# Gateloop attention with a multiplicative FFN: score and state products as 32-column blocks, a second copy of v, and a new place for the weight looks

## The chip, the cores and the metric

The kernel runs on one core of one Trainium2 chip. The metric is the device time in microseconds of one launch, as the median of several runs. Three runs of the kernel before gave 569.23, 569.44 and 571.16 us, so its time is 569.44 us.

## What is computed

The input is q, k, v and a complex gate a = (a_re, a_im), each 4 x 8 x 768 x 48 (batch, heads, sequence, head size) in fp32, and four weight matrices in fp64. For each batch and head a 48 x 48 complex state is multiplied, row by row, by the gate of the step and gets k v^T added; the output is q times the real part of the state. The outputs of all heads, as rows of 384, then go through an FFN that multiplies two projections with each other:

```python
mag = sqrt(a_re * a_re + a_im * a_im)
a_re, a_im = (x * min(mag, 0.999) / (mag + 1e-6) for x in (a_re, a_im))
for t in range(S):
    new_re = ar * S_re - ai * S_im
    new_im = ar * S_im + ai * S_re
    S_re, S_im = new_re + outer(k[t], v[t]), new_im
    y[t] = q[t] @ S_re
x = y.transpose(0, 2, 1, 3).reshape(B * S, H * D)      # 3072 x 384
out = ((x @ w1) * (x @ w2)) @ w3 @ w_out               # 384 -> 1024 -> 1024 -> 384
```

## The kernel before, in words

The sequence of a batch is cut into two halves of 384 steps. A half is a unit; there are NU = 8 units, each with UC = 3 chunks of C = 128 steps, for all 8 heads. The cumulative product of the gates turns the recurrence into products of matrices: with the gates' running product folded into q and k, the output of a chunk is a causal score product times v plus q times the state at the chunk's start.

**Start.** w3 and w_out are turned from fp64 to fp32 on VectorE and ScalarE and multiplied with each other into w3o (`row_work`, `fuse`, L973), so that the FFN needs one matrix less; w1 and w2 follow (`w12_work`, `load_weight`, L873 to L887). The gates of unit 0 and the first products of unit 0 are worked in between. `load_v` is called when row `VLOAD` (3) of w3 is reached.

**A unit** (`unit`, `pieces`) works on these things:

- `gates(u + 1)` (L541): the gates of the next unit, a chain of steps that goes back and forth between ScalarE (L554: Ln, Exp, Arctan, Sin) and VectorE (L566 to L638: products and scans over time). It ends with `gR` (L634), k (L635), gA and q (L637, L638), and with DMAs that move these into head order as KL and QL (L648). `turn` needs gR and k; `scores` needs KL and QL. Near its end it calls `spread_v` (L520), two copies on ScalarE that bring v from the loaded tile `vr` into `V`, with 64 columns a head where 48 are data and 16 stay zero.
- `turn` (L664): the transposes `tp` (L671) of three 128 x 128 blocks and a copy on ScalarE into KT (L673).
- `state` (L714): for each of 8 heads a product kv (L721) with a stationary operand of 96 columns (real and imaginary parts of k) and 64 moving columns (v), then an addition on VectorE into T (L728), at the end of a unit also a multiplication by the decay (L734). The second unit of a batch needs only two of them.
- `scores` (L676): for 4 heads a product sc (L683) with 96 rows, 128 stationary columns (k) and 128 moving ones (q), into one PSUM bank; then VectorE copies the causal part into A with a mask (L685). Two such calls make a chunk. Two banks take turns.
- `outputs` (L691): y (L710), all in the narrow form of TensorE: the stationary operand has 32 columns, and four such blocks, with outputs on PSUM partitions 0, 32, 64 and 96, are issued one after another (`lanes`). ScalarE copies the result into xT (L712).
- the FFN of the unit before, in between as filling: `ffn_ab` (L737) with 96 instructions m (L744) and a multiplication on VectorE (L750); `ffn_out` (o, L831); and `out_pair` (p, L795), seven half-size products that replace eight for two blocks of rows.
- `look` (`check_weights`, L899): 42 steps that test whether the inputs are in the range for which the fast way is sound: 6 of the gates, 36 of the fp64 weights. A step is a DMA, then two or three passes on ScalarE (L918 to L921, or L527). `judge` (L979) adds up all tests and the end of the kernel reads the verdict; a general way (`general`) stands behind it and isn't taken here.

**Order.** PE's order is written out by hand (`manual_schedule`): it is the order of the calls in `unit` and in the main part. The other engines' order is set by a scheduler from the order of calls and from priorities. Each engine then works strictly in its order. All DMAs are issued by SP, one after another, also in the scheduler's order; one that must wait for its buffer holds up those behind it. In `unit` each call of a piece is followed by a step of `gates`, and each piece by a step of `look`:

```python
for i in range(n):
    for f in rest[first[i]:first[i + 1]] + p[i]:
        f()
        next(steps, None)
    next(look, None)
```

## Time and profile before

| what | value |
|---|---|
| median of 3 runs | 569.44 us |
| span of the profiled execution, first to last instruction | 566.8 us |
| its own time over the span | not recorded apart; the median lies 2.6 us above the span |
| mean granted TensorE clock | 0.995 |
| PE busy | 541.8 us, 3682 matmul instructions |
| VectorE / ScalarE / GpSimd busy | 335.8 / 345.9 / 3.5 us |
| m (L744) | 768 instructions, 135.0 + 134.3 us |
| sc (L683) | 384 instructions, 47.2 us |
| kv (L721) | 320 instructions, 30.0 us |
| y (L710) | 1408 instructions, 39.2 + 34.4 us, interleaved |
| V copies (L524) | 16, 10.5 us |
| DMA queue | 46720 packets, 84.06 MB |

The page of the profile is of one execution. Busy time of an engine is the union of its instructions' times; for PE the ends of matmuls are modelled, and matmuls overlap, so the start-to-start distances in the chain and the timeline say more than the busy times. In lines of the groups, "x384 | 45.7, 192 | 1.3" reads: 384 instructions, 45.7 us busy in all, 192 ns each on average, 1.3 us of idle time of the engine just before them, followed by what ended it. In the chain, each line is its start in us, its length in us, and what was running.

### The profile page before, as it was taken

What the parts mean: (1) busy time and instruction counts of PE and PEld (TensorE: products, weight loads), DVE (VectorE), ACT (ScalarE), POOL (GpSimd) and SP (SyncE); (2) the same over time, 40 slices, a digit from 0 to 9 for tenths busy, and PEclk for the clock granted to TensorE, in tenths of its full rate; (3) what the DMA queues carried; (4) which work ended last, traced back from release to release, by engine and by line L of the source; (5) the groups of instructions that cost most, each with busy time, mean ns of one, the idle gap of its engine ahead of it and who ended that gap; (6) DMA issues with size and microseconds to landing.
All of it is one profiled execution on the core that took longest, in us unless ns stands there. A gap on an engine that the chain in (4) does not pass through costs nothing.

```text
span 566.8 us, 9285 instructions
## 1 busy us (share of the span) xinstructions
PE 541.8 (96%) x3682; PEld 386.1 (68%) x3682; DVE 335.8 (59%) x511; ACT 345.9 (61%) x569; POOL 3.5 (1%) x9
## 2 busy tenths in 40 slices
PE   4697899999999999999999999999999999999995
PEld 2354775577566975688567966697568965796564
DVE  6998599927752677356742796255743696332121
ACT  6979856655662798458963899289965645101100
POOL 2000000000000000000000000000000000000000
PEclk9999999999999999999999999999999999999999
DMA  8996985780382447935593427754393104200001
GB/s 285 374 364 190 322 268 169 204 214 16 98 189 53 122 141 221 247 109 183 184 206 111 144 81 218 209 157 148 125 207 101 30 28 115 67 2 30 0 1 47
DMA packets 46772, 84.74 MB, mean 150 GB/s; under 512 B 4736, under 2 KB 36480, under 8 KB 45952
## 3 DMA queue, kind: packets, MB, share of 16 engines
q1 hardware_dynamic: 46720, 84.06, 50.6%
q8 instruction: 31, 0.51, 0.4%
q14 instruction: 21, 0.17, 0.1%
HBM read 60.42 MB, written 4.72 MB: 115 GB/s over the span
## 4 chain that ended last, share of the span: by engine, by line
PE 77%; ACT 9%; DVE 7%; DMA 3%; issue 2%; SPq 1%; DVEq 0%; ACTq 0%
PE m L744 40%; PE o L831 9%; PE p L795 9%; PE y L710 5%; PE sc L683 5%; PE kv L721 5%; PE tp L671 2%; ACT gZ L554 1%; DMA look<-in_w_dram 1%; ACT look L918 1%; ACT look L919 1%; PE f L973 1%; DMA im<-in_a_im_dram 1%; ACT gR L554 1%; ACT gA L554 1%
## 5 line engine op out<-in xcount | busy, mean ns | idle before, releaser
L744 PE MATMUL m<-xT,w1s 128*128 128x384 f32 x384 | 135.0, 488 | 0.1
L744 PE MATMUL m<-xT,w2s 128*128 128x384 f32 x384 | 134.3, 486 | 0.0
L744 PEld LDWEIGHTS m<-xT,w2s 128*128 128x128 f32 x384 | 73.0, 190 | 50.9
L744 PEld LDWEIGHTS m<-xT,w1s 128*128 128x128 f32 x384 | 71.2, 190 | 45.3 <-ACT xT L712 1.0
L750 DVE TENSOR_TENSOR ab<-m,a 128x384 f32<-128x384 f32 x64 | 35.2, 553 | 84.7 <-PE m L744 77.4
L749 ACT COPY a<-m 128x384 f32<-128x384 f32 x64 | 30.1, 474 | 53.5 <-PE m L744 52.3
L973 PE MATMUL f<-wo_s,w3s 128*128 128x384 f32 x128 | 47.7, 528 | 15.5 <-DVE wo_s L887 15.5
L831 PE MATMUL o<-w3o,ab 128*128 128x384 f32 x160 | 54.0, 487 | 0.0
L673 ACT COPY KT<-tp 128x384 f32<-128x384 f32 x40 | 33.6, 851 | 32.2 <-PE tp L671 32.1
L973 PEld LDWEIGHTS f<-wo_s,w3s 128*128 128x128 f32 x128 | 25.5, 206 | 35.2 <-DVE wo_s L887 18.6
L683 PE MATMUL sc<-QL,KL 96*128 96x128 f32 x384 | 47.2, 276 | 0.3 <-DVE A L685 0.3
L683 PEld LDWEIGHTS sc<-QL,KL 96*128 96x128 f32 x384 | 45.7, 192 | 1.3 <-DVE A L685 0.6
L685 DVE COPY_PREDICATED A<-causal,sc 128x512 f32<-128x512 int32 x48 | 34.6, 741 | 14.0 <-PE sc L683 13.6
L831 PEld LDWEIGHTS o<-w3o,ab 128*128 128x128 f32 x160 | 29.6, 190 | 18.7 <-issue 0.4
L728 DVE TENSOR_TENSOR T<-kv,T 96x512 f32<-96x512 f32 x16 | 11.0, 686 | 51.4 <-PE kv L721 51.4
L710 PE MATMUL y<-A,V 128*32 128x128 f32 x768 | 39.2, 275 | 0.0
L710 PEld LDWEIGHTS y<-A,V 128*32 128x32 f32 x768 | 32.9, 109 | 3.3 <-issue 1.4
L710 PE MATMUL y<-QL,T 96*32 96x128 f32 x640 | 34.4, 272 | 0.0
L877 ACT ACTIVATE low<-raw 128x384 uint16<-128x384 uint32 (+4 forms) x28 | 25.1, 902 | 11.1 <-DVE low L873 5.1
L721 PEld LDWEIGHTS kv<-V,KT 128*96 128x96 f32 x320 | 29.6, 165 | 3.1 <-issue 1.4
L795 PE MATMUL p<-To,So 128*128 128x192 f32 x168 | 31.6, 335 | 0.0
L721 PE MATMUL kv<-V,KT 128*96 128x64 f32 x320 | 30.0, 247 | 1.5 <-ACT KT L673 1.5
(114 smaller groups left out, 748.7 us busy)
## 6 DMA issues: line engine op xcount, KB each, us to landing
look<-in_w_dram SPq DMA_DIRECT2D x28, 512.0 KB, 3.9
raw<-in_w_dram SPq DMA_DIRECT2D x6, 1024.0 KB, 10.2
raw<-in_w_dram SPq DMA_DIRECT2D x8, 768.0 KB, 6.7
KL<-gR SPq DMA_DIRECT2D x24, 192.5 KB, 3.3
KL<-k SPq DMA_DIRECT2D x24, 192.5 KB, 3.8
re<-in_a_re_dram SPq DMA_DIRECT2D x24, 192.0 KB, 5.2
im<-in_a_im_dram SPq DMA_DIRECT2D x24, 192.0 KB, 3.2
k<-in_k_dram SPq DMA_DIRECT2D x24, 192.0 KB, 3.3
```

Source lines behind the costliest of these rows:

```text
L673: nc.scalar.copy(out=KT_t[u, c][:, :, :, x].rearrange("p h d f -> p f d h"), in_=tp.rearrange("p f (d h) -> p f d h", h=H))
L683: nc.tensor.matmul(out=sc[:, j], lhsT=KL[:, x * n + j, w], rhs=QL[:, x * n + j, w], start=True, stop=True)
L685: masked[:] = [nc.vector.copy_predicated(out=A[:, x * n:(x + 1) * n], data=sc, mask=causal.rearrange("p (h t) -> p h t", h=1).to_broadcast ...
L710: nc.tensor.matmul(out=o, lhsT=a, rhs=b, start=s0, stop=s1)
L721: nc.tensor.matmul(out=kv[:, hd], lhsT=KT[:, hd].rearrange("p d x f -> p (d x f)"), rhs=V[:, hd], start=True, stop=True)
L744: nc.tensor.matmul(out=m, lhsT=w[:, j * P // WB, f, j * P % WB:j * P % WB + P], rhs=xT_t[u][:, f], start=(f == 0), stop=(f == KD - 1))
L749: copied[:] = [nc.scalar.copy(out=a, in_=got[0])]
L750: nc.vector.tensor_tensor(out=ab_t[u][:, j], in0=got[1], in1=a, op=OP.mult)
L795: nc.tensor.matmul(out=m[p], lhsT=a[:, f], rhs=b[:, f], start=(f == 0), stop=(f == KH - 1))
L831: nc.tensor.matmul(out=m, lhsT=ab_t[u][:, f, t * P:(t + 1) * P], rhs=w3o[:, f], start=(f == 0), stop=(f == KF - 1))
L877: nc.scalar.activation(out=ends.bitcast(U16)[:, 0::2].rearrange("p (r m) -> p r m", r=r), in_=lo.bitcast(U32), func=AF.Copy, scale=2.0 ** -29)
L973: nc.tensor.matmul(out=sums[j], lhsT=w3_t[f][:, j * P:(j + 1) * P], rhs=w3_t["wo"][:, f], start=(f == 0), stop=(f == KF - 1))
```

## The change

It has four parts.

1. **Scores in blocks.** Each 128 x 128 score product is cut into four with 32 stationary columns each. Block s0 needs the query steps from s0 on alone, so the moving columns are 128, 96, 64 and 32. Each block's output goes to one of the four groups of 32 PSUM partitions, chosen so that the four heads of a call stand in four different groups. The rows of a head's scores so are rotated by 32 times its number modulo 4; the mask is laid out to match (now 8 bits, made once for four heads), the two score banks are fixed tiles that are zeroed at the start, and the rows of v in `V` are rotated in the same way.
2. **States in blocks.** Each 96-column state product is cut into three with 32 columns, in three groups. v comes unrotated from `vr`, with 48 moving columns where there were 64. T has three fixed tiles, zeroed once, and 48 columns of each head are written.
3. **v twice.** `vr` is loaded as before, but a unit's load is now called after the last state of the unit before. `turn_v` loads v a second time from memory, straight into `V`, rotated, head by head: 14 DMAs a unit with runs of 192 bytes. `spread_v` is gone.
4. **Looks.** A unit takes a look after each of its first four pieces alone (the last unit after every piece); the remaining ones are taken in the last FFN, and `judge` comes four calls before its end.

The diff, with the plain renamings left out:

```diff
@@ -427,8 +428,10 @@
     TT = S // 2
     UC = TT // C
     NU = 2 * B
+    LOOKS = 4
     AHEAD = [0, 0] + [4] * (NU - 2)
     LO, HI = 32, D - 32
+    SB, LANES = 32, C // 32
     LN_EPS = math.log(1e-6)
     PI = math.pi
     MIN_SQ, MAX_SQ = 1.126 ** 2, 2.0 ** 32 - 512
@@ -446,8 +449,7 @@
     singles = fast.enter_context(tc.tile_pool(name="singles", bufs=1))
     one = fast.enter_context(tc.tile_pool(name="one", bufs=1))
     two = fast.enter_context(tc.tile_pool(name="two", bufs=2))
-    three = fast.enter_context(tc.tile_pool(name="three", bufs=3))
-    ps_s = fast.enter_context(tc.tile_pool(name="ps_s", bufs=2, space=PSUM))
+    ps_s = fast.enter_context(tc.tile_pool(name="ps_s", bufs=1, space=PSUM))
     ps_v = fast.enter_context(tc.tile_pool(name="ps_v", bufs=2, space=PSUM))
     ps_m = fast.enter_context(tc.tile_pool(name="ps_m", bufs=4, space=PSUM))
@@ -455,13 +457,19 @@
     gate_pool = [one, None]
+    Sc = [ps_s.tile([P, LANES, C], FP, name=f"sc{i}") for i in range(2)]
+    for sc in Sc:
+        nc.vector.memset(sc, 0.0)
     Ab = [singles.tile([P, H, C], FP, name=f"A{i}") for i in range(2)]
     Vb = [singles.tile([P, UC, H, 64], FP, name=f"V{i}") for i in range(2)]
-    causal = singles.tile([P, C], I32, name="causal")
-    nc.gpsimd.iota(causal, pattern=[[1, C]], base=0, channel_multiplier=-1)
-    nc.vector.tensor_scalar(out=causal, in0=causal, scalar1=0, scalar2=None, op0=OP.is_ge)
+    causal = one.tile([P, LANES, C], I32, tag="q", name="causal")
+    nc.gpsimd.iota(causal, pattern=[[SB, LANES], [1, C]], base=0, channel_multiplier=-1)
+    for j in range(1, LANES):
+        nc.vector.tensor_scalar(out=causal[0:SB * j, j], in0=causal[0:SB * j, j], scalar1=-C, scalar2=None, op0=OP.add)
+    mask = singles.tile([P, LANES, C], U8, name="mask")
+    nc.vector.tensor_scalar(out=mask, in0=causal, scalar1=0, scalar2=None, op0=OP.is_ge)
     consts = singles.tile([P, 7], FP, name="consts")
     for i, x in enumerate((1.0, LN_EPS, PI / 2, SMALL, -LARGE, MIN_SQ, -MAX_SQ)):
         nc.vector.memset(consts[:, i:i + 1], x)
@@ -506,8 +514,6 @@
         g = g_t[u]
         load_rows(g["k"], kt, u)
         load_rows(g["q"], qt, u)
-        if u:
-            load_v(u)
     def load_v(u):
         b, h = divmod(u, 2)
@@ -517,11 +523,14 @@
         nc.sync.dma_start(out=vr, in_=v[b, h * TT:(h + 1) * TT].rearrange("(c p) e -> p c e", p=C))
         g_t[u]["vr"] = vr
-    def spread_v(u):
-        vr = g_t[u]["vr"].rearrange("p c (h two d) -> p c h two d", two=2, d=D)
-        V = Vb[u % 2].rearrange("p c (h two) e -> p c h two e", two=2)
-        for i, e0 in enumerate((0, 64 - D)):
-            nc.scalar.copy(out=V[:, :, :, i, e0:e0 + D], in_=vr[:, :, :, i])
+    def turn_v(u):
+        b, h = divmod(u, 2)
+        src = v[b, h * TT:(h + 1) * TT].rearrange("(c p) (h d) -> p c h d", p=C, d=D)
+        for hd in range(H):
+            r = SB * (hd % LANES)
+            for p0, p1, s0 in ((r, C, 0), (0, r, C - r)):
+                if p1 > p0:
+                    nc.sync.dma_start(out=Vb[u % 2][p0:p1, :, hd, 0:D], in_=src[s0:s0 + p1 - p0, :, hd])
     def check_gates(u, re, junk, f=0):
         return [nc.scalar.activation(out=junk, in_=re, func=AF.Relu, scale=scale, bias=bias,
@@ -603,8 +612,6 @@
             tt(out=k[:, s], in0=k[:, s], in1=r[:, s], op=OP.mult)
         for X in (R[:, :, TT], K2[:, :, TT], st_dec[:, u]):
             nc.scalar.copy(out=X, in_=A[:, :, TT - 1])
-        if u:
-            spread_v(u)
         yield
         chain(nc.scalar.preload_act_table_set("trig_and_small"))
         for s in parts:
@@ -678,15 +685,24 @@
         w = slice(c * C, (c + 1) * C)
         A = Ab[(u * UC + c) % 2]
         n = H // 2
-        sc = ps_s.tile([P, n, C], FP, tag="sc", name="sc")
-        for j in range(n):
-            nc.tensor.matmul(out=sc[:, j], lhsT=KL[:, x * n + j, w], rhs=QL[:, x * n + j, w], start=True, stop=True)
+        sc = Sc[x]
+        for s0 in SPANS:
+            for j in range(n):
+                g = (s0 // SB + j) % LANES
+                nc.tensor.matmul(out=sc[SB * g:SB * g + SB, j, s0:C], lhsT=KL[:, x * n + j, w][:, s0:s0 + SB],
+                                 rhs=QL[:, x * n + j, w][:, s0:C], start=True, stop=True)
         with tc.high_priority():
             masked[:] = [nc.vector.copy_predicated(out=A[:, x * n:(x + 1) * n], data=sc,
-                                      mask=causal.rearrange("p (h t) -> p h t", h=1).to_broadcast([P, n, C]))]
+                                      mask=mask)]
+    SPANS = (0, 3 * SB, SB, 2 * SB)
     QUADS = [q for h in range(0, H, 2) for q in ([(h, 0)], [(h, 1), (h + 1, 0)], [(h + 1, 1)])]
+    def part(X, hd, e):
+        e0 = 64 * hd + 32 * e - (64 - D) * (hd % 2)
+        return X.rearrange("p h e -> p (h e)")[:, e0:e0 + 32]
     def outputs(u, c):
         QL = L_t[u][0]
@@ -701,9 +717,9 @@
         for i, q in enumerate(QUADS):
             f, j = divmod(i, 4)
             o = y[32 * j:32 * j + 32, f]
-            got = [(V[:, hd, 32 * e:32 * e + 32], A[:, hd]) for hd, e in q]
+            got = [(part(V, hd, e), A[:, hd]) for hd, e in q]
             if not first:
-                got += [(T[:, hd, 32 * e:32 * e + 32], QL[:, hd, w]) for hd, e in q]
+                got += [(part(T, hd, e), QL[:, hd, w]) for hd, e in q]
             lanes[j] += [(o, a, b, n == 0, n == len(got) - 1) for n, (a, b) in enumerate(got)]
         for step in zip(*lanes):
             for o, a, b, s0, s1 in step:
@@ -711,28 +727,35 @@
         with tc.high_priority():
             nc.scalar.copy(out=xT_t[u][:, :, w], in_=y)
+    Tb = [singles.tile([2 * D, H, 64], FP, name=f"T{i}") for i in range(3)]
+    for T in Tb:
+        nc.gpsimd.memset(T, 0.0)
     def state(u, c):
-        KT, V = KT_t.pop((u, c)), Vb[u % 2][:, c]
+        KT, V = KT_t.pop((u, c)), g_t[u]["vr"][:, c].rearrange("p (h d) -> p h d", d=D)
         n = u % 2 * UC + c
         T = T_t.get((u // 2, n))
-        kv = ps_v.tile([2 * D, H, 64], FP, tag="v", name="kv")
+        kv = ps_v.tile([2 * D, H, D], FP, tag="v", name="kv")
         for hd in range(H):
-            nc.tensor.matmul(out=kv[:, hd], lhsT=KT[:, hd].rearrange("p d x f -> p (d x f)"), rhs=V[:, hd],
-                             start=True, stop=True)
-        Tn = three.tile([2 * D, H, 64], FP, tag="T", name="T")
+            rows = KT[:, hd].rearrange("p d x f -> p (d x f)")
+            for g in range(0, 2 * D, SB):
+                nc.tensor.matmul(out=kv[g:g + SB, hd], lhsT=rows[:, g:g + SB], rhs=V[:, hd], start=True, stop=True)
+        Tn = Tb[(u * UC + c) % 3]
         with tc.high_priority():
             if T is None:
-                nc.scalar.copy(out=Tn, in_=kv)
+                nc.scalar.copy(out=Tn[:, :, 0:D], in_=kv)
             else:
-                add = nc.vector.tensor_tensor(out=Tn, in0=kv, in1=T, op=OP.add)
+                add = nc.vector.tensor_tensor(out=Tn[:, :, 0:D], in0=kv, in1=T[:, :, 0:D], op=OP.add)
                 if (u, c) == (0, 1):
                     tc.add_manual_dep(add.ins, begun[-1].ins.name, ORDER, reason="begun")
         if c == UC - 1:
-            rho = L_t[u][1][:, :, TT:TT + 1].to_broadcast([2 * D, H, 64])
-            nc.vector.tensor_tensor(out=Tn, in0=Tn, in1=rho, op=OP.mult)
+            rho = L_t[u][1][:, :, TT:TT + 1].to_broadcast([2 * D, H, D])
+            nc.vector.tensor_tensor(out=Tn[:, :, 0:D], in0=Tn[:, :, 0:D], in1=rho, op=OP.mult)
         T_t[u // 2, n + 1] = Tn
+        if u + 1 < NU and c == UC - 1 - u % 2:
+            load_v(u + 1)
     def ffn_ab(u, j):
         if j == 0:
@@ -967,7 +990,7 @@
     def fuse(f, j):
         if not sums:
-            sums.extend([ps_s.tile([P, DM], FP, tag="sc", name="f") for _ in range(2)] +
+            sums.extend([sc.rearrange("p n t -> p (n t)")[:, 0:DM] for sc in Sc] +
                         [ps_v.tile([P, DM], FP, tag="v", name="f") for _ in range(2)] +
                         [ps_m.tile([P, DM], FP, tag="mm", name="f") for _ in range(4)])
         nc.tensor.matmul(out=sums[j], lhsT=w3_t[f][:, j * P:(j + 1) * P], rhs=w3_t["wo"][:, f], start=(f == 0),
@@ -990,7 +1013,7 @@
             need += m
             nc.vector.scalar_tensor_tensor(out=ok[:, 0:m], in0=t, scalar=x, in1=ONE.to_broadcast([P, m]), op0=op,
                                            op1=OP.mult, accum_out=tot[:, i:i + 1])
-        m = ps_m.tile([P, TT], FP, tag="mm", name="count")
+        m = ps_v.tile([P, TT], FP, tag="v", name="count")
         nc.tensor.matmul(out=m[0:1, 0:6], lhsT=ONE, rhs=tot, start=True, stop=True)
         count = singles.tile([1, 7], FP, name="count")
         nc.vector.scalar_tensor_tensor(out=count[:, 0:6], in0=m[0:1, 0:6], scalar=1.0, in1=ONE[0:1].to_broadcast([1, 6]),
@@ -1036,7 +1059,8 @@
             for f in rest[first[i]:first[i + 1]] + p[i]:
                 f()
                 next(steps, None)
-            next(look, None)
+            if i < LOOKS or u == NU - 1:
+                next(look, None)
     gate_pool[1] = fast.enter_context(tc.tile_pool(name="late_gates", bufs=1))
     with tc.manual_schedule(engines={mybir.EngineType.PE}):
@@ -1057,6 +1081,7 @@
                 row_load(f + 4)
             if f == VLOAD:
                 load_v(0)
+                turn_v(0)
             if f >= KF - 2:
                 continue
             for j in range(KF):
@@ -1066,7 +1091,6 @@
         work = w12_work()
         for _ in steps:
             pass
-        spread_v(0)
         for f in work[:2]:
             f()
         for f in range(KF - 2, KF):
@@ -1086,6 +1110,7 @@
                 for f in work[:2]:
                     f()
                 load_qkv(1)
+                turn_v(1)
             for _ in range(5 if i == 0 else i >= 6):
                 next(steps)
             if i in (5, 7):
@@ -1105,15 +1130,20 @@
         look = check_weights(fast.enter_context(tc.tile_pool(name="looks", bufs=2)))
         out_weights()
         for u in range(1, NU):
+            if u + 1 < NU:
+                turn_v(u + 1)
             steps = gates(u + 1, False) if u + 1 < NU else iter(())
             unit(u, steps, rest[HEAD:] if u == 1 else ffn(u - 1), look if u > 1 else iter(()), AHEAD[u])
             for _ in steps:
                 pass
-        for _ in look:
-            pass
-        judge()
-        for f in ffn(NU - 1, 2):
+        end = ffn(NU - 1, 2)
+        for i, f in enumerate(end):
             f()
+            next(look, None)
+            if i == len(end) - 4:
+                for _ in look:
+                    pass
+                judge()
     fast.close()
     value = nc.values_load(good[0:1, 0:1], min_val=0, max_val=1)
```

## The prediction

> **What bounds the kernel now.** First the page: span, busy times, slices, queue.
>
> ```profile
> span 566.8 us, 9285 instructions
> ...
> PE 541.8 (96%) x3682; PEld 386.1 (68%) x3682; DVE 335.8 (59%) x511; ACT 345.9 (61%) x569; POOL 3.5 (1%) x9
> ...
> PE   4697899999999999999999999999999999999995
> ...
> DMA  8996985780382447935593427754393104200001
> ...
> q1 hardware_dynamic: 46720, 84.06, 50.6%
> ```
>
> A slice is 14.2 us. From the sixth (71 us) TensorE is at 9 without a break. Busy is no proof, so second the chain of waits in order of time, whose pieces run start to start:
>
> ```profile
> 81.82 30.96 PE m L744 x96
> ...
> 128.33 1.89 PE y L710 x64
> ...
> 134.79 3.65 PE y L710 x128
> ...
> 182.95 1.33 PE kv L721 x16
> ...
> 190.44 1.30 PE p L795 x8
> 191.74 1.79 PE sc L683 x16
> 193.53 1.01 PE y L710 x32
> 194.54 1.50 PE p L795 x8
> ```
>
> The reader is to see PE piece after PE piece with no hole. So a nanosecond off PE after 82 us is a nanosecond off the end, as long as the others keep up. The code has 192 score matmuls (8 heads, 3 chunks, 8 units) and the groups list 384: an fp32 matmul is two instructions, each with its own weight load. I call load and matmul a pair. Third, the weight loads, in the groups kept apart by shape (last numbers: mean ns, idle before):
>
> ```profile
> L683 PEld LDWEIGHTS sc<-QL,KL 96*128 96x128 f32 x384 | 45.7, 192 | 1.3 <-DVE A L685 0.6
> L710 PEld LDWEIGHTS y<-A,V 128*32 128x32 f32 x768 | 32.9, 109 | 3.3 <-issue 1.4
> L721 PEld LDWEIGHTS kv<-V,KT 128*96 128x96 f32 x320 | 29.6, 165 | 3.1 <-issue 1.4 <-ACT KT L673 1.2
> ```
>
> A load grows by (192 - 109) / 96 = 0.86 ns a column: 111, 83 and 28 ns for 128, 96 and 32 columns above a latency of about 81. A matmul streams at 30.96 us / 96 / 384 = 0.84 ns a column; in y, (3.65 - 1.89) / 64 = 27.5 ns a pair, four column groups at once, is 110 ns for 128 columns: 0.86. So sc (1.79 / 16 = 112 ns) sits at both limits, and kv (1.33 / 16 = 83 ns) at its 96-column load; its 64 columns stream in 55. Fourth, the start of a y in the timeline:
>
> ```profile
> 128.26 0.16 PEld L710 LDWEIGHTS y<-A,V 128*32 128x32 f32 x8
> 128.26 0.32 PE L710 MATMUL y<-A,V 128*32 128x128 f32 x4
> ```
>
> Eight loads of 0.11 us fit into 0.16: their starts lie within 0.05 us. One after another at 28 ns they would need 0.2. So column groups load, and stream, beside each other, and a pair can start every 7 ns or so.
>
> [...] p costs 1.50 after y and 1.30 after sc, and 64 pairs of y take 1.89, not 64 x 27.5 = 1.76. A stay in the narrow mode so costs 0.20 + 0.13 = 0.33 us. [...]
>
> **The change part by part.**
>
> Scores. A chunk was 16 pairs of 128 columns, 1.79 us. It becomes two sets of four rounds (128, 32, 96, 64 columns), each round two pairs in each of four groups: 2 x 2 x 320 x 0.86 = 1.10 us; the 32-column round, 27.5 ns, just covers four starts at 7 and a load of 28. Saved 0.69 a chunk.
>
> States. 16 pairs, 1.33 us, become 16 rounds of three groups with 48 columns: 16 x 48 x 0.86 = 0.66, above the 28 of a load. Saved 0.67; of these there are 20 (three in even units, two in odd).
>
> Units 1 to 7: 21 x 0.69 + 17 x 0.67 = 25.9 us. Unit 0 (57 to 82 us) waits on other engines as well: of 3 x 0.69 + 3 x 0.67 = 4.1 I count 2.0.
>
> Mode changes. So far only y is narrow, three stays in most units. The first two kv, and the stretch kv+sc or sc ahead of the first p, become stays of their own: three more in each of units 2 to 7, one in unit 1 (where scores follow each other), two in unit 0: 21 x 0.33 = 6.9 us lost.
>
> Bounds of a pair. No row shows narrow pairs back to back. From 7 ns (then the above holds) to 27.5, y's (sc 64 x 27.5 = 1.76, kv 48 x 27.5 = 1.32, nothing saved). I take the low end, since eight loads did start in 0.05 us.
>
> ScalarE. The spread of v goes: 16 copies of 664 ns, 10.5 us, 1.3 a unit, off the path but in its queue. The looks are moved: 42 steps, so far one a piece and done by unit 6; now four a unit in units 2 to 6, ten in unit 7, the rest in the last products. The profile shows what they cost today:
>
> ```profile
> PE tp L671 <- DVE gR L634: 1.4, 1, 1.4
> ...
> 252.36 1.19 ACT look L918 x2
> 253.55 0.78 ACT look L919 x2
> 254.34 3.50 DMA look<-in_w_dram
> ```
>
> The first (waits) is PE waiting for the next unit's gates, once, at 411 us; the rest (chain) are looks, and a load for one, in the queue that makes the gates. In the other units from 2 on, gR (L634, in the timeline) ends 0.6 to 6 us before the transposes ask for it, so the gates follow TensorE closely. The units get about 2.5 us shorter: without relief they would be late every time. Relief: by the order of instructions two looks stay within the gates where four to nine stood (a look is 1.65 to 2.6 us of ScalarE by its rows), the V copies go, and the tests of L991 (1.2 us in the last gates) move to the tail. I count the 1.5 won back, and 2.5 new: 0.8 in unit 1, where two chunks of scores share the two score banks without a product between, the rest late gates. In the tail the count's matmul waits for the last look; p and o (9 us) cover it; I count 0.5 (0 to 2).
>
> VectorE. The masks keep their size (741 ns; the new mask's type I count at nothing, the p of 1.3 us between products covers it; uncovered it would delay each chunk by what a mask grows); the T adds shrink from 512 to 384 columns, some 0.13 us each, off the path. Two memsets (A's 0.91 us halved each) and the mask are done while the first weights land; T is zeroed on GpSimd, 1% busy.
>
> DMA and SP. The second v is 14 DMAs a unit, 3072 runs of 192 B. At 0.6 us an issue (three of re take 1.83) SP spends 8.4 us a unit. In units 1 to 6 what is behind them on SP are out rows, k, q and im, due ten us later or more; SP waits 90 us for rows of ot anyway. The plain load of v gains a wait, for the unit's last kv; in even units k and q queue behind it, from about 188 us in unit 2, and L602 asks for q at 207. The looks' loads move with them; in the tail they stand before the last out rows, and ScalarE frees their buffers some us earlier. The first stands behind vr at 29.8 us, where SP then waits until 41.5 for the gates: it fits, with unit 1's re and im and the KL moves behind it. The second stands after q (66 us) and ahead of the third pair of w1/w2 loads, issued at 74.6: it just fits. Bytes alone: 84.06 MB in 50.6% of 16 x 566.8 us are 18.3 B/ns an engine, so 0.59 MB take 2.0 us; [...] if each took a mean packet's 98 ns, 18.8. I take 4: the slice after 42.5 us shows 6, some 5.7 us free. Cost 0; if the cover is gone, see below.
>
> Sum: -25.9 - 2.0 + 6.9 - 1.5 + 2.5 + 0.5 = -19.5 us. The profiled span of 566.8 becomes 547.3. The median, 569.4, lies 2.6 above the span (its start and end are outside), so **550**.
>
> **The rivals.**
>
> A pair has a floor (slower). If narrow pairs cost what y's do, 27.5 ns, sc gives 24 x (1.79 - 1.76), kv 20 x (1.33 - 1.32), about 1 us; the mode changes stay, 6.9: 575. It decides from (24 x 1.79 + 20 x 1.33 - 6.9) / (24 x 64 + 20 x 48) = 25 ns a pair, where gain and loss are even. For it: [...] 5500 TensorE instructions where there were 3682. Against it: the start of y. A floor of 20 ns: sc 4 x (110 + 80 + 82.5 + 80) = 1.41, kv 0.96, saved 24 x 0.38 + 20 x 0.37 = 16.5, less 6.9: 560.
>
> The gates become the bound. If six units each stall by another 1.5 us, 9 are given back: 559. For it: the 0.6 to 2 us of slack. Against: the looks taken out.
>
> The second v hurts. At 18.8 us a unit it delays KL, QL and the first w1/w2 blocks: past the 5.7 us free, up to 13 come back: 563.
>
> That nothing changes isn't possible: the shapes in the order of instructions differ.
>
> **How the numbers follow.** Forecast (544 to 556): 0.60. Gates, v, or a floor near 20 (556 to 566): 0.20. A floor near 24 (566 to 572): 0.07. The full floor (572 to 580): 0.13. About 0.5% is what a measurement of this kernel tells from no change. So faster 0.80, same 0.07, slower 0.13. The range from 544 to 570 leaves out the slow floor and a little below.
>
> **What would show it.** Right: in the chain sc near 1.1 us a chunk and kv near 0.7 a run, p after kv or sc at 1.5, y as before; no V copy and two looks in the gates' stretch; no wait on DMA after 60 us. Wrong: sc at 1.7 (floor), waits of tp on gR in every unit (gates), PE idle between 60 and 100 us (v).

## The result, and the profile after

In eight runs each, the changed kernel took 563.52 us in the median (562.30 to 568.42) and the kernel before 569.52 us (568.58 to 573.61). The ratio is 0.990, with an interval from 0.987 to 0.993. The forecast was 550 us, with a range from 544 to 570: the direction is right, but of 19.5 us only some 6 came. The profiled execution has a span of 560.9 us (before: 566.8), so 13.6 us of the forecast of 547.3 are missing. Every run also reports its time beside its span: the time lies about 1.6 us above the span in the changed kernel and 1.8 in the kernel before, not 2.6; the profiled execution of before was some 0.8 us faster than the median. It has a granted clock of 0.995, while 55 of the 83 others on record have 0.993 or less; that of the changed kernel, 0.985, is the middle of its eight.

The page of the changed kernel, the lines that answer to those of before:

```profile
span 560.9 us, 13020 instructions
...
PE 525.6 (94%) x5474; PEld 359.5 (64%) x5474; DVE 333.8 (60%) x516; ACT 341.2 (61%) x553; POOL 5.3 (1%) x12
...
PE   4798789999999999999999999998999999998995
...
PEclk9899889999999999999999999999999999998998
DMA  8996978786464541964292634873491207256441
...
q1 hardware_dynamic: 73088, 88.79, 57.7%
q8 instruction: 45, 0.74, 0.6%
```

TensorE is busy for 16 us less, but the span lost only 6: the rest turned into idle time. New holes are in the slices 5 and 6 (56 to 84 us), at 379 to 393 us and at 505 to 519 us; in the first two and the last of these slices the row of the granted clock shows 8 as well.

The chain of waits, in order of time, in unit 2:

```profile
183.62 0.81 PE kv L743 x48
184.43 1.50 PE p L818 x8
...
188.38 1.32 PE sc L692 x58
189.70 1.50 PE p L818 x8
191.20 1.25 PE sc L692 x64
192.46 0.88 PE y L726 x32
193.33 1.50 PE p L818 x8
194.83 1.25 PE sc L692 x64
196.09 1.76 PE y L726 x64
197.84 1.50 PE p L818 x8
```

A state run takes 0.81 us (1.33 before) with its mode change, a chunk of scores 1.25 (1.79). The latter is read here as containing part of a mode change; in the timeline, 1.14 us lie between the start of a chunk's scores and that of the y right behind them, which has the same narrow form (191.13 and 192.27 us). The first p after kv or sc is at 1.50, y is unchanged. These are the sizes that the forecast named. The weight loads, kept apart by shape:

```profile
L726 PEld LDWEIGHTS y<-A,V 128*32 128x32 f32 x768 | 33.6, 110 | 1.3 <-issue 1.3
L692 PEld LDWEIGHTS sc<-QL,KL 96*32 96x32 f32 x1536 | 29.8, 113 | 12.6 <-issue 5.1 <-DVE A L695 2.9 <-DMA QL<-q 2.2
L743 PEld LDWEIGHTS kv<-vr,KT 128*32 128x32 f32 x960 | 14.9, 110 | 6.2 <-issue 4.3 <-ACT KT L680 1.4 <-ACT gA L563 0.5
```

The loads of sc and kv now last as long as those of y, but the idle time before the loads of sc rose from 1.3 to 12.6 us. The waits of TensorE (total, times, longest) say for what:

```profile
PE sc L996 <- DVE wo_s L910: 14.5, 5, 7.6
PE m L767 <- ACT xT L728: 5.3, 3, 2.6
PE sc L692 <- DVE A L695: 2.2, 2, 1.9
PE sc L692 <- DMA QL<-q: 2.0, 1, 2.0
PE sc L692 <- issue: 1.4, 3, 0.7
PE y L726 <- issue: 1.3, 2, 0.7
```

The first line belongs to the start (L996 is the product of w3 and w_out, written into a score bank) and is about as long as before (15.5). The others are new or longer: the kernel before had only 3.2 us in waits apart from the first, 1.5 for KT, 1.4 for gR and 0.3 for A. The wait for gR that the forecast watched is gone; m waits for xT instead, a copy on ScalarE.

The stretches between the first gated pieces m of successive units show where it stands (us; first column: start of the first m):

```text
                first m | to the next m, units 1 to 7               | last m to last TensorE
before            81.65 | 61.98 62.11 61.21 62.21 61.17 63.80 61.16 | 45.49
after             83.37 | 61.31 59.19 60.83 60.74 60.88 59.29 61.27 | 47.63
```

Units 2 and 6 are clean: 2.9 us shorter than units 2 and 4 before (unit 6 before, at 63.80, had the wait for gR). Units 1, 3, 4, 5 and 7, the start and the tail are not.

### The profile page after: what moved, and what is told of

Same layout as the page of the kernel before. It is cut to its first block, busy times and chain, and to the rows that moved or that the text cites. A ratio compares the mean times of both kernels' runs of the same rounds, so it can differ in the third digit from the quotient of the medians.

```text
span 560.9 us, 13020 instructions
## 1 busy us (share of the span) xinstructions
PE 525.6 (94%) x5474; PEld 359.5 (64%) x5474; DVE 333.8 (60%) x516; ACT 341.2 (61%) x553; POOL 5.3 (1%) x12
## 4 chain that ended last, share of the span: by engine, by line
PE 68%; DVE 10%; DMA 9%; ACT 7%; issue 4%; SPq 2%; DVEq 0%; ACTq 0%
PE m L767 39%; PE p L818 9%; PE o L854 7%; PE y L726 5%; PE sc L692 4%; DMA k<-in_k_dram 2%; PE kv L743 2%; DMA look<-in_w_dram 2%; PE tp L678 2%; ACT low L900 2%; DVE gA L599 1%; DMA V<-in_v_dram 1%; DMA re<-in_a_re_dram 1%; DMA look<-in_w_out_dram 1%; DMA KL<-k 1%
## 5 line engine op out<-in xcount | busy, mean ns | idle before, releaser
L767 PE MATMUL m<-xT,w1s 128*128 128x384 f32 x384 | 136.8, 493 | 5.3 <-ACT xT L728 5.3
L695 DVE COPY_PREDICATED A<-mask,sc 128x512 f32<-128x512 uint8 x48 | 33.2, 731 | 11.8 <-PE sc L692 11.3
L692 PE MATMUL sc<-QL,KL 96*32 96x64 f32 (+3 forms) x1536 | 34.5, 241 | 5.8 <-DVE A L695 2.2
L692 PEld LDWEIGHTS sc<-QL,KL 96*32 96x32 f32 x1536 | 29.8, 113 | 12.6 <-issue 5.1
L726 PE MATMUL y<-QL,T 96*32 96x128 f32 x640 | 35.6, 272 | 1.4 <-issue 1.3
L996 PE MATMUL f<-wo_s,w3s 128*128 128x384 f32 x96 | 36.3, 525 | 0.0
L563 ACT ACTIVATE re<-gZ 128x1152 int32<-128x1152 f32 (+2 forms) x17 | 17.8, 1048 | 30.0 <-DVE gZ L622 21.3
L749 DVE TENSOR_TENSOR T<-kv,T 96x384 f32<-96x384 f32 x16 | 8.8, 553 | 42.3 <-PE kv L743 42.2
L563 ACT ACTIVATE gR<-gA 128x1152 f32<-128x1152 f32 (+1 forms) x20 | 19.3, 967 | 23.5 <-DVE gA L599 23.4
L726 PEld LDWEIGHTS y<-QL,T 96*32 96x32 f32 x640 | 31.4, 110 | 2.2 <-issue 2.2
```

What stands on the lines that cost most here:

```text
L563: chain(nc.scalar.activation(**kw))
L692: nc.tensor.matmul(out=sc[SB * g:SB * g + SB, j, s0:C], lhsT=KL[:, x * n + j, w][:, s0:s0 + SB], rhs=QL[:, x * n + j, w][:, s0:C], start=T ...
L695: masked[:] = [nc.vector.copy_predicated(out=A[:, x * n:(x + 1) * n], data=sc, mask=mask)]
L726: nc.tensor.matmul(out=o, lhsT=a, rhs=b, start=s0, stop=s1)
L767: nc.tensor.matmul(out=m, lhsT=w[:, j * P // WB, f, j * P % WB:j * P % WB + P], rhs=xT_t[u][:, f], start=(f == 0), stop=(f == KD - 1))
L996: nc.tensor.matmul(out=sums[j], lhsT=w3_t[f][:, j * P:(j + 1) * P], rhs=w3_t["wo"][:, f], start=(f == 0), stop=(f == KF - 1))
```

## The experiments

All times are medians, the ratios are to the kernel before on the same chip, with a 95% interval. The change itself is at 0.990 [0.987, 0.993]: where a run's interval overlaps this one, the medians alone don't tell the two apart. Each trace is of one execution. In seven kernels whose edits leave the start alone (the change and experiments 4, 5, 6 and 10) the first m starts anywhere from 82.70 to 85.06 us, so a difference of one or two us in this number shows nothing by itself.

**1. Products whole, everything else changed (blocks_undone).** The rows of v and the mask are unrotated to match.

```diff
-        for s0 in SPANS:
-            for j in range(n):
-                g = (s0 // SB + j) % LANES
-                nc.tensor.matmul(out=sc[SB * g:SB * g + SB, j, s0:C], lhsT=KL[:, x * n + j, w][:, s0:s0 + SB],
-                                 rhs=QL[:, x * n + j, w][:, s0:C], start=True, stop=True)
+        for j in range(n):
+            nc.tensor.matmul(out=sc[:, j], lhsT=KL[:, x * n + j, w], rhs=QL[:, x * n + j, w], start=True, stop=True)
...
-            for g in range(0, 2 * D, SB):
-                nc.tensor.matmul(out=kv[g:g + SB, hd], lhsT=rows[:, g:g + SB], rhs=V[:, hd], start=True, stop=True)
+            nc.tensor.matmul(out=kv[:, hd], lhsT=rows, rhs=V[:, hd], start=True, stop=True)
```

> All of the change but its narrow products: scores are again one product of 128 stationary columns a head, states one of 96 (48 moving columns), the mask and the second load of v are not rotated, v is still loaded twice with the same 14 DMAs and the looks stay where the change puts them. Theory A (the second load of v and the looks cost time of their own): slower than the kernel before, 572 to 577 us, with PE waiting between 57 and 85 us and in the last unit. Rival B (they cost nothing; what is late is only late because TensorE got faster): 567.5 to 570.5 us, the time of the kernel before. In both, sc is back at 1.79 us a chunk and kv at 1.33 a run.

Measured: 574.34 us, ratio 1.007 [1.005, 1.010], as theory A has it. The companions of the change cost 4.8 us by themselves, and the narrow products bring 10.8. In the profiled execution, at 577.32 us the slowest of the six, the first m starts at 85.20 us, 3.5 later than before, and the tail has the 47.7 us of the changed kernel.

**2. and 3. One product narrow at a time (kv_only, sc_only).** Each undoes one of the two hunks above and keeps the other product narrow.

> The change with narrow states and whole scores (128 columns, rows of v and mask not rotated, v loaded in the same 14 DMAs). If each product's gain adds up on TensorE as the trace has it (sc 1.79 to 1.14 us a chunk, less 0.33 a stay in the narrow mode): 571 to 574 us, nearly all of the gain is the scores'. If the other engines take back what TensorE gains, whichever product gives it: 566 to 569 us.

Measured: 571.01 us, ratio 1.003 [1.001, 1.005].

> The change with narrow scores and whole states (one product of 96 columns a head, 48 moving columns, 1.33 us a run). If the gains add up: the states give 20 x (1.33 - 0.81) less the modes' 0.2 a run, about 6 us, so 568 to 571 us. If the other engines take back what TensorE gains: 563 to 566 us.

Measured: 569.99 us, ratio 1.001 [0.999, 1.002]. Beside whole products (574.3) the narrow states bring 3.3 us, the narrow scores 4.3, both together 10.8: more than the sum, though each time lies in the range expected if the gains add up, or at its edge. A reason that fits a part of it is the mode change, which kv and the sc behind it share when both are narrow and each pays when alone: in the traces, units 2 to 7 get shorter by 4.4 us with narrow states alone, 5.6 with narrow scores alone and 11.3 with both, 1.3 more than the sum, and three shared stays at the forecast's 0.33 us would be 1.0. The rest of the surplus stays open.

**4. Looks after every piece, as before (looks_back).**

```diff
-            if i < LOOKS or u == NU - 1:
-                next(look, None)
+            next(look, None)
...
-        end = ffn(NU - 1, 2)
-        for i, f in enumerate(end):
-            f()
-            next(look, None)
-            if i == len(end) - 4:
-                for _ in look:
-                    pass
-                judge()
+        for _ in look:
+            pass
+        judge()
+        for f in ffn(NU - 1, 2):
+            f()
```

> The change with the looks where the kernel before had them: one after every piece, none in the last products, the tests added up ahead of the last FFN. If the new place of the looks is what holds TensorE up in the units (xT behind looks): 557 to 560 us. If the old place would be worse, because five to nine looks stand in the queue that makes the gates, now that TensorE is faster: 566 to 571 us, with waits of tp on gR in units 3 to 6.

Measured: 561.33 us, ratio 0.984 [0.981, 0.987]: 2.2 us better than the change by the medians (the two intervals just touch), and between the two expectations. The tail is back at 45.49 us; units 2 to 7 take 361.9 us in sum (362.2 with the change), with 3.1 us of waits of tp for gR in place of some of those for xT. So in these two executions the new place of the looks relieved the units by next to nothing, and cost 2.1 in the tail.

**5. No looks at all (looks_out).** This kernel leaves the 42 tests of the inputs out.

```diff
-        look = check_weights(fast.enter_context(tc.tile_pool(name="looks", bufs=2)))
+        look = iter(())
```

> The change with all 42 looks left out (the tests of the weights and of the first two units' gates are not made; the output is the same). Theory A (looks ahead of the xT copies and in the tail hold TensorE up, and the last one halves its clock for a while): 555 to 558 us, waits of m on xT gone. Rival B (the gates' own chain is the bound at TensorE's new pace): 561 us or more, the waits of m on xT stay.

Measured: 557.94 us, ratio 0.978 [0.974, 0.981]. Unit 7 falls from 61.27 to 58.52 us and the tail to 45.7. The time is that of theory A, but of the waits of m on xT only unit 7's is gone: units 3 and 5 stay at 60.6, and m still waits 2.6 us for xT there. So not the looks hold these, but something else in ScalarE's queue.

**6. The last copy ahead of the logarithm (xt_first).** On ScalarE, the logarithm of the running product, a step of the next unit's gates, is put behind the unit's last turned copy.

```diff
         for s in parts:
             act(out=r[:, s], in_=A[:, s], func=AF.Ln)
+            behind[u] = chained[-1]
...
-            nc.scalar.copy(out=xT_t[u][:, :, w], in_=y)
+            xt = nc.scalar.copy(out=xT_t[u][:, :, w], in_=y)
+        if u > 1 and c == UC - 1 and u + 1 in behind:
+            tc.add_manual_dep(behind[u + 1].ins, xt.ins.name, ORDER, reason="xT first")
```

> The change with one order added on ScalarE: the step of the next unit's gates that waits for the scans (the logarithm of the running product) goes behind the last xT copy of the unit. Theory (m of the next FFN waits for xT because that step, itself waiting for VectorE, stands ahead of it): the stretches from one FFN to the next that took 60.8, 60.7 and 60.9 us lose 1 to 2 us each, the wait of m on xT falls from 5.3 us to 2.6 (that of the last unit, which has looks ahead of it), and the time is 559 to 561.5 us. Rival (the gates are then late instead, and tp waits for gR): 562.5 us or more.

Measured: 561.94 us, ratio 0.987 [0.985, 0.990], between the two expectations and not told apart from the change by the medians; the wait of m on xT falls from 5.3 us to 4.9 only, not to 2.6. ScalarE around the end of unit 3, of the changed kernel (start us, length us, instruction, idle time before it and what ended that):

```profile
263.12 1.16 ACT L563 ACTIVATE gR<-gA 128x1152 f32<-128x1152 f32 x1 [3.92 <-DVE gA L599]
264.19 0.46 ACT L728 COPY xT<-y 128x384 f32<-128x384 f32 x1
264.55 1.17 ACT L563 ACTIVATE gR<-gR 128x1152 f32<-128x1152 f32 x1
```

and of this one:

```profile
263.04 0.20 ACT L616 COPY gR<-gA 128x3 f32<-128x3 f32 x1 [3.92 <-DVE gA L600]
263.14 0.19 ACT L616 COPY k<-gA 128x3 f32<-128x3 f32 x1
263.24 0.47 ACT L730 COPY xT<-y 128x384 f32<-128x384 f32 x1
263.61 1.16 ACT L564 ACTIVATE gR<-gA 128x1152 f32<-128x1152 f32 x1
```

In this stretch ScalarE worked in the order of its program: it waited 3.92 us for VectorE's scan of the gates, and the copy, at 264.19 us, stood behind that wait although its y was long done (at 260.78 us). The edit brings the copy 0.95 us earlier, 0.8 of it by the start of the unit, and units 3 and 5 fall by 0.8 and 0.9 us to 60.02 and 59.99. But two small copies that need the same scan still stand in front, so the wait of 3.92 us itself is not taken out of xT's way. In the kernel before, ScalarE had another order at this place, with the copy ahead of the logarithm and no idle time before it:

```profile
265.87 0.66 ACT L524 COPY V<-vr 128x576 f32<-128x576 f32 x1
266.43 0.47 ACT L712 COPY xT<-y 128x384 f32<-128x384 f32 x1
266.92 1.17 ACT L554 ACTIVATE gR<-gA 128x1152 f32<-128x1152 f32 x1
```

So what put this copy behind the scan is the order that ScalarE got with the change, not TensorE's pace alone. Why the scheduler chose it isn't recorded, and no run puts the copy ahead of all that needs the scan.

**7. The second v issued later (v_later).** `turn_v(0)` comes after the moves of KL and QL, `turn_v(1)` after the FFN products of unit 0.

```diff
                 load_v(0)
-                turn_v(0)
...
         for _ in steps:
             pass
+        turn_v(0)
...
                 load_qkv(1)
-                turn_v(1)
...
         out_weights()
+        turn_v(1)
         for u in range(1, NU):
```

> The change with the second load of v of unit 0 called after the moves of KL and QL, and that of unit 1 after unit 0's FFN, so that re, im and the moves are no longer behind 14 DMAs on SP. Theory A (those 14 DMAs are what delays the start): m of the first FFN starts at 79 to 81 us rather than at 83.4, 559 to 561 us in all. Rival (the DMAs' own data, or w1/w2 now behind them, cost as much): 562.5 to 566 us.

Measured: 565.16 us, ratio 0.992 [0.990, 0.995]. The first m stays at 83.64 us. The rival has it. TensorE's wait for QL is gone, but kv now waits 2.1 us for KT (1.1 with the change), and a stop for "issue" of 1.6 us comes at 81 us.

**8. No second v for units 0 and 1 (v01_out),** without the two calls; what it leaves out stands in the expectation.

> The change without the second load of v for units 0 and 1 (28 of the 112 DMAs; the first batch's output is not that of the reference, all instructions on the engines stay). Theory A (these DMAs are what delays the start): m of the first FFN starts at 79 to 81 us rather than at 83.4, sc no longer waits for the move of q, and the time is 559 to 561 us. Rival (the start is late for another reason, such as the new mask, the zeroing of the score banks, or unit 0's steps waiting for each other): m starts at 83 us or later and the time stays at 562.5 to 565 us.

Measured: 563.73 us, ratio 0.992 [0.989, 0.995]; the first m at 84.74 us, both as the rival has it. The loads alone don't hold the start: the wait for QL is gone here too, and in its place are 2.1 us for KT and two stops for "issue" of 1.9 and 1.7 us. What the loads do to SP is plain in its own queue, in the changed kernel

```profile
31.07 0.39 SPq L523 DMA_DIRECT2D vr<-in_v_dram  x1
32.08 16.58 SPq L533 DMA_DIRECT2D V<-in_v_dram  x14
48.76 1.84 SPq L495 DMA_DIRECT2D re<-in_a_re_dram  x3
50.65 1.88 SPq L495 DMA_DIRECT2D im<-in_a_im_dram  x3
52.63 0.63 SPq L655 DMA_DIRECT2D KL<-gR  x1
```

and before:

```profile
29.84 0.43 SPq L517 DMA_DIRECT2D vr<-in_v_dram  x1
41.54 1.83 SPq L487 DMA_DIRECT2D re<-in_a_re_dram  x3
43.41 1.88 SPq L487 DMA_DIRECT2D im<-in_a_im_dram  x3
45.39 1.51 SPq L648 DMA_DIRECT2D KL<-gR  x1
```

Fourteen issues take 16.6 us, with pauses between them, instead of the 8.4 of the forecast, and unit 1's gate loads and the moves of KL are issued 7.2 us later. The DMA engines have no free time when these issues begin (a share of 1.00 or more from 28 to 44 us); for units 2 to 7 the same fourteen take 9.1 to 10.3 us.

**9. Whole products, and no second v for units 0 and 1 (v01_whole).** Experiments 1 and 8 together.

> Score and state products whole, as before, and no second loading of v for units 0 and 1 (their state products of the other blocks read what is left in the buffer, so the output of these units is not the reference's; units 2 to 7 load it as in the changed kernel). Theory: the late start of the sequence of units is shared by two things that each suffice, the fourteen early loads on SP and TensorE's pause with the halved clock; with whole products and without the loads both are gone, so the first gated piece starts at 81.5 to 82.5 us as before, and the time is 570.5 to 573 us (574.3 less some 3). Rival: something else of the change's new order of work delays the start (the looks at the weights, or the order of the loads), and the first gated piece stays at 84 to 85.5 us and the time at 573.5 to 575 us.

Measured: 573.11 us, ratio 1.005 [1.003, 1.007], between the two expectations; the first m at 84.68 us, in an execution of 576.44 us, the slowest of the seven. TensorE around 68 us, of this kernel

```profile
66.92 1.71 PE L737 MATMUL kv<-vr,KT 128*96 128x48 f32 x16 [0.92 <-ACT KT L678]
68.43 3.75 PE L688 MATMUL sc<-QL,KL 96*128 96x128 f32 x16
71.97 2.77 PE L990 MATMUL f<-wo_s,w3s 128*128 128x384 f32 x4
```

and of the kernel before:

```profile
66.78 1.57 PE L721 MATMUL kv<-V,KT 128*96 128x64 f32 x16 [0.92 <-ACT KT L673]
68.19 2.00 PE L683 MATMUL sc<-QL,KL 96*128 96x128 f32 x16
70.03 1.46 PE L973 MATMUL f<-wo_s,w3s 128*128 128x384 f32 x4
```

Both come to sc at the same time to within 0.24 us. Then the same products take nearly twice as long: from 68.2 us the granted clock is 0.5 for 6.8 us. By the first m 3.03 us are lost, so in this execution nearly all of the delay is the clock. Whether the faster ones start late as well is not recorded.

**10. The three improvements put together (back_first, six_first, out_first).** back_first joins experiments 4 and 6. six_first takes looks in the first six pieces, with experiment 6. out_first leaves all looks out, with experiment 6.

```diff
-    LOOKS = 4
+    LOOKS = 6
```

> The looks at the weights after every piece, none in the tail, and the logarithm of the running product behind the unit's last turned copy on ScalarE. If the two stalls are separate, what each brought alone adds up: 2.2 us (looks) and 1.6 us (turned copy) off 563.5, so 559 to 560.5 us, the odd units at 60.0 instead of 60.8 us and the tail at 45.5. Rival: the looks that come back take the place that the copy has just gained, since ScalarE is in order, and the time stays at 561 to 562 us.

Measured: 560.83 us, ratio 0.983 [0.981, 0.984]; units 3 and 5 61.42 and 60.50, tail 45.49. Between the two expectations. That the looks take part of the place that the copy gained is likely, but not shown: unit 3 also has a wait of 1.3 us for gR and a stop for "issue" of 0.9 us.

> Looks in the first six pieces of a unit instead of four, and the logarithm behind the last turned copy. With twelve more looks done by unit 6, fewer are left for unit 7 and the tail: the tail goes from 47.7 to 45.5 to 46.5 us, the copy's order gains the 1.6 us that it gained alone, and the time is 559 to 560.5 us. Rival: the looks in the fifth and sixth piece hold the turned copies and masks of those pieces, the units grow by some 0.3 us each, and the time is 561 to 562.5 us.

Measured: 558.96 us, ratio 0.981 [0.979, 0.983], tail 45.81, unit 7 60.13. This is the fastest kernel that computes everything: 4.6 us below the change, by the medians. Unit 2 does grow, from 59.19 to 60.62, as the rival has it; in the traces the gain is in units 3, 5 and 7, the start, and the tail, which has no half clock in this execution.

> No looks at the weights at all (they are left out of the computation) and the logarithm behind the last turned copy: what is left is the products, the gates and the start. If ScalarE's order is what holds units 3 and 5, they come from 60.6 us (looks left out alone) down to 59.2 to 59.9, and the time is 555.5 to 557 us; if VectorE's own queue of gates and masks holds them, they stay at 60.5 and the time at 557.5 to 558.5 us.

Measured: 555.88 us, ratio 0.975 [0.973, 0.977]; units 3 and 5 at 59.76, as ScalarE's order would have it. That is not all of their stall: a clean odd unit takes 58.52 (unit 7 of experiment 5), and m still waits 1.1 and 0.4 us for xT, which stands behind the scan here too.

**11. Work for TensorE in the pause ahead of 67 us (fill, six_fill).** The last state product of unit 0 is computed three times over.

```diff
-        for hd in range(H):
+        for hd in list(range(H)) * (3 if (u, c) == (0, 2) else 1):
```

> The changed kernel, with the last state product of unit 0 computed three times over (the same values into the same place), which gives TensorE 1.3 us of work in the 2 us in which it waits for QL ahead of 67 us. Theory: it is the pause that makes the clock fall to 0.5 for 6.8 us from 66 us on; with the filler it stays at 1 there, the first gated piece starts at 80.5 to 82 us instead of 83.4, and the time is 560.5 to 562 us. Rival: VectorE and ScalarE are late there anyway, so that even at the full clock the piece starts at 83 to 84 us and the time stays at 563 to 564 us. If the clock falls all the same, the run doesn't tell.

Measured: 564.13 us, ratio 0.989 [0.986, 0.993]. The clock stays at 1 in the profiled execution, but the first m starts at 86.01 us, later than with the pause. TensorE (the bracket is idle time before the line):

```profile
68.59 0.62 PE L743 MATMUL kv<-vr,KT 128*32 128x48 f32 x29 [3.12 <-issue]
...
75.73 0.86 PE L692 MATMUL sc<-QL,KL 96*32 96x64 f32 x35 [3.08 <-issue]
...
80.28 0.25 PE L692 MATMUL sc<-QL,KL 96*32 96x64 f32 x2 [1.72 <-issue]
```

TensorE stops three times in the middle of a run of products, waiting for nothing that the program made. Counting TensorE's instructions from the start, its waits for semaphores along with the loads and matmuls, the stops stand behind numbers 705, 961 and 1217: 256 apart. And the queue that the profile calls "instruction" moves a 16 KB packet that ends 1.4 us ahead of the end of each:

```text
stop of fill   behind no.  ends at   last 16 KB packet: start, length
3.12 us        705         68.59     66.1, 1.1
3.08 us        961         75.73     73.0, 1.3
1.72 us        1217        80.28     77.5, 1.4
```

From these places and packets the stops are read here as TensorE waiting for instructions that the next packet brings; how many it holds at a time no run shows. six_fill is the same on six_first:

> The same filler with looks in the first six pieces of a unit and the logarithm behind the last turned copy. Theory: no halved clock around 66 us, the first gated piece at 80 to 81.5 us instead of 82.7, and 556.5 to 558 us instead of 559.0. Rival: 82.5 to 83.5 us and 558.5 to 559.5 us.

Measured: 562.38 us, ratio 0.987 [0.983, 0.991], first m at 85.99 us, stops of 2.8, 1.4 and 2.3 us; here the clock did fall, for 3.4 us (mean 0.991). The expectations of both runs failed in the same new way.

**12. The same bridge in few instructions (fill_wide, six_wide, v01_fill).** One whole state product, 32 instructions where fill has 192.

```diff
+        if (u, c) == (0, 2):
+            for hd in range(H):
+                nc.tensor.matmul(out=kv[:, hd], lhsT=KT[:, hd].rearrange("p d x f -> p (d x f)"), rhs=V[:, hd], start=True,
+                                 stop=True)
```

> The changed kernel, with the last state product of unit 0 computed a second time, in the whole 96-column form (the same values into the same place): 1.3 us of work for TensorE ahead of the wait for QL in 32 instructions, where the run fill had 192. If the fetch of instructions stopped the run fill, the stops of 3 us at 65, 73 and 79 us are gone or below 1 us. Then, if the clock stays at 1 as there, the first gated piece starts at 80.5 to 82.5 us and the time is 560.5 to 562.5 us. Rival: VectorE and ScalarE are late anyway; the piece starts at 83 to 84.5 us and the time is 563 to 564.5 us. If the stops stay at 3 us, the fetch isn't the reason.

Measured: 562.17 us, ratio 0.988 [0.985, 0.991]. The stop at number 705 is 1.32 us instead of 3.12, a little more than expected, the one at 961 is gone, that at 1217 is 0.74. With 32 instructions in place of 192 the stops so get shorter or go, which bears out the reading as a wait for instructions. The clock stays at 1 around 66 us in the profiled execution (the fastest of the four, at 0.994; the others have 0.986), and yet the first m starts at 83.69: TensorE now waits 3.4 us ahead of it for VectorE's masks (A), 1.9 with the change, which stand in a queue with the conversions of w1 and w2. The rival has it for the start, though the time lies in the theory's range.

> The same bridge of 32 instructions with looks in the first six pieces and the logarithm behind the last turned copy. Theory (fetch and clock): no stop over 1 us for issue, no halved clock around 66 us, the first gated piece at 80 to 82 us instead of 82.7, and 556.5 to 558.5 us instead of 559.0. Rival: 82.5 to 84 us and 559 to 560.5 us.

Measured: 561.56 us, ratio 0.986 [0.984, 0.988], first m at 84.75 us in the slowest of the five executions (564.53): slower than without the bridge (558.96), and there the clock fell at 70.6 us all the same (mean 0.987). Both parts of this expectation failed.

> The changed kernel without the second loading of v for units 0 and 1 (the output of these units is not the reference's) and with the state product of 32 instructions ahead of the wait for QL. If the loads and the pause each suffice to hold the start, both are gone now and the first gated piece starts at 79.5 to 81.5 us, and the time is 559 to 561.5 us. Rival: the conversions of w1 and w2 on VectorE and ScalarE, or the loads that they wait for, set it: 83 to 84.5 us and 562 to 563.5 us.

Measured: 564.41 us, ratio 0.991 [0.988, 0.994], first m at 84.47 us. The clock fell at 66.1 us (mean 0.989) in spite of the bridge, which TensorE reached only after a wait of 2.1 us, and a stop for "issue" of 1.9 us came behind number 1217, so this run doesn't settle it.

## Why the prediction was right or wrong

**The products: right.** The forecast had 1.10 us a chunk and 0.66 a state run, plus 0.33 a stay in the narrow mode; measured were 1.14 from a chunk's scores to the y behind them, 0.81 for a state run with its stay, and 1.50 for the next p. A pair costs 17 to 18 ns. In units 2 to 7 the change would save 18.4 us if all were clean: three even units of 59.24 (mean of units 2 and 6) and three odd ones of 58.52 (unit 7 with the looks left out), in sum 353.3 instead of the 371.7 before. The forecast for these, stalls apart, was 18.0. The floor rival is out, at its 27.5 ns and at the 25 where gain and loss would be even: 17.8 ns (1.14 us / 64) for 80 moving columns on average and the 27.5 ns of y for 128 are 0.89 and 0.86 ns a column in four groups, so y's figure went with its columns and was not a floor.

**The step that failed: "I count the 1.5 won back, and 2.5 new".** Units 2 to 7 take 362.2 us, so they lose 8.9 us to stalls (counted: 1.7), and unit 1, which gained 0.7 where 2.3 were forecast, another 1.6. Apart from 0.8 us in unit 1, the forecast looked for stalls only where the next unit's gates meet the transposes. In the changed kernel's trace they are:

- **xT behind other work on ScalarE**, 5.2 us: 1.12 and 1.54 in units 3 and 5 (behind the logarithm and the scan that it waits for, experiment 6), 2.58 in unit 7 behind a look whose DMA came late:

```profile
505.81 0.65 ACT L941 ACTIVATE look<-look 128x512 f32<-128x512 f32 x1 [1.54 <-DMA look<-in_w_dram]
506.36 0.46 ACT L728 COPY xT<-y 128x384 f32<-128x384 f32 x1
```

  The rival "the gates become the bound" had the right pair of engines for units 3 and 5, but neither the place nor the size (six stalls of 1.5 us; here two, 2.7 us in sum). It looked at tp waiting for gR. The gates were late in another way: ScalarE waited for VectorE inside them, and a finished product waited behind ScalarE.
- **Stops for instructions**, as read above, 2.7 us from unit 1 on, 1.0 of them in unit 1: stops of 0.30 to 0.72 us for "issue" at 128.3, 137.8, 250.5, 316.6 and 374.6 us, all behind a number that is 193 more than a multiple of 256, as 705, 961 and 1217 are. The kernel before has none at such a number. The forecast read the 5500 instructions only as a matter of time per pair; that TensorE can stop at places 256 of them apart, and that 256 of them now last some 2.3 us in the scores (128 pairs at 17.8 ns) where they lasted 14 in whole ones (16 pairs in 1.79 us), was no term of the sum.
- Some 2 us in units 2 to 7 lie in no idle time that the trace shows, and stay open, as do 0.6 of unit 1's 1.6.

**"Unit 0 … I count 2.0" and the second v at "Cost 0": wrong by 3.1 us together.** The first m was to start at 80.3 us (2.0 less two stays) and starts at 83.4. The term of SP was mis-sized: 16.6 us for 14 issues, not 8.4 (the 4 us for the transfers were the author's estimate, and no run shows them apart). The wait for QL (2.0 us at 67 us, where the forecast had "no wait on DMA after 60 us") follows from it: it is gone in experiments 7 and 8. But taking the loads away (8), delaying them (7), or bridging the pause (12) frees nothing that the spread of 82.7 to 85.1 us would let one see: each time another wait ends about as late. What the runs show is a set of waits that take each other's place: QL, VectorE's conversions and masks, the stops for "issue", and the clock. Which of them must go together is not settled; experiment 12's last run was to tell and didn't. Shown is only that with whole products and no early v the start is as before up to 68 us, and in one slow execution then loses 3 us to the clock. Some of the 3.1 us may be luck as well: the kernel before was profiled once, in an execution with a better clock than most of its others.

**The tail at 0.5: 2.1.** "p and o (9 us) cover it" was true of the count's matmul (it waits 0.3 us), but 1.6 of the 2.1 us are the clock. The wait of unit 7 for xT, above, was followed by 3.4 us at half the clock, at the start of the tail, and the 96 m there took 32.52 us; without looks (30.96 us for the m, a tail of 45.7) this interval is absent. It is absent too in four runs that have the looks where the change has them (v01_out, fill, fill_wide, v01_fill), though m waits there as well, for 2.0 to 3.4 us: their tails are 45.9 to 46.4 us, 0.4 to 0.9 above the kernel before. So the looks' own cost is near the forecast, and what it left out is the clock, for which the sum has no term. The granted clock in both places (length, busy time and number of instructions of the engines, clock, DMA share, GB/s), in the changed kernel:

```profile
66.10:72.90 6.80, 5.76 (x88) 3.81 (x92) 5.25 (x10) 5.19 (x5) 0.00 (x0) 0.50 1.04 375
...
503.00:506.40 3.40, 1.29 (x8) 0.99 (x7) 0.98 (x3) 1.83 (x6) 0.00 (x0) 1.00 0.73 207
506.40:509.80 3.40, 2.92 (x5) 1.72 (x6) 0.00 (x0) 3.06 (x8) 0.00 (x0) 0.51 0.51 177
```

Over its eight runs the changed kernel has a median clock of 0.985, the kernel before 0.992 over 83. If the clock is either 1 or 0.5, as in the traces, a mean lower by 0.007 is half speed for another share of 2 x 0.007 of 561 us: 7.9 us, at most 3.9 us of time, an estimate.

**The sum again.** Of the 13.6 us missing in the span, 3.1 lie ahead of the first m, 1.6 in unit 1, 6.9 in units 2 to 7 (16.3 forecast, 9.5 measured), 1.6 in the tail and 0.5 behind TensorE's last product (6.4 us to the end of the span instead of 6.0). The time falls into the 556 to 566 us that the forecast gave a chance of 0.20, for late gates, a costly second v or a floor near 20 ns; pairs at 17 to 18 ns leave no such floor, and gates and v did cost time, but each in another place than named.

## What to carry to other kernels

When the bounding engine gets faster by a twentieth (here 2.9 of 62.2 us a unit), price not only whether the others keep up on average, but each place where a finished result waits behind another's wait in an in-order queue: here a 0.46 us copy behind a 3.9 us wait. Cutting products into pieces multiplies instructions, and at 17 to 18 ns a pair TensorE here also stopped for 0.30 to 0.72 us from unit 1 on, idle time put down to "issue", at places a multiple of 256 instructions apart: look for such places, and count them. A short pause of the bounding engine can cost again: the waits of 2.0 us for QL and 2.6 us for xT here went with 6.8 and 3.4 us at half the clock. And a stage that varies by 2 us from execution to execution (the first m, 82.70 to 85.06 us) is not judged by one trace each.

## What the runs showed of the hardware

- Narrow fp32 products in different column groups ran at 16.9 to 17.8 ns a pair (48 pairs in 0.81 us, 64 in 1.14), with loads of 110 to 113 ns each that so lay beside each other, those of one run all in the same rows. The whole p took 1.50 us right behind narrow products and 1.30 behind whole ones: 0.20 us for the change.
- TensorE stopped at places 256 instructions apart: in fill for 3.12, 3.08 and 1.72 us, in fill_wide for 1.32 and 0.74 us at two of them, in the changed kernel from unit 1 on for 0.30 to 0.72 us at five places, multiples of 256 apart. Around 65 us in fill, with the DMA engines busy throughout (a share of 1.09), a 16 KB packet of the queue "instruction" came 4.7 us after the 256 instructions before it were begun, took 1.1 us, and TensorE went on 1.4 us after its end; at the five later stops of the changed kernel the packet came 1.1 to 2.8 us after, and TensorE went on 1.3 to 1.6 us after its end.
- The granted clock was 0.50 for 6.8 us from 66.1 us and 0.51 for 3.4 us from 506.4 us in the changed kernel, and 0.50 for 6.8 us from 68.2 us in v01_whole. In the 3.4 us ahead of these TensorE was busy for 1.25, 1.29 and some 2.5 us (37%, 38% and 73%). How short or how long a pause it takes isn't shown: the stop of 3.12 us in fill, ahead of 68.59 us, was not followed by half clock, and at the end of unit 7 a wait for xT of 2.6 us in the changed kernel was, but waits of 3.4 us in fill and 2.9 in v01_out were not.
- The issue of a small DMA of v on SP took from 0.3 to 3.1 us between 32 and 49 us, in a stretch that begins with the DMA engines busy throughout.
